# First MLP's input kept in SBUF: attention's output evicted into the contraction's rows, two heads moved by DMA within SBUF

## The chip, the cores and the metric

The kernel runs on one core of a Trainium2 chip. The metric is the device time of one execution in microseconds, the median of three runs. TensorE is the matrix engine, VectorE (DVE) and ScalarE (ACT) do elementwise work, GpSimd (POOL) is all but unused, and SyncE (SP) issues every DMA. TensorE's clock is granted at one of two levels, 1.2 GHz (0.50 in the profile) and 2.4 GHz (1.00).

## The reference

A gated linear attention is followed by two MLPs over the same 3072 tokens.

```python
# batch 4, heads 8, seq 768, head_dim 48
f = 1 / (1 + exp(-f_logit))
for t in range(S):
    state = f[t][:, None] * state + outer(k[t], v[t])
    y[t] = q[t] @ state
x = y as rows of 3072 tokens by 384 (8 heads x 48)
# first MLP, d_ff 2048
h = x @ w1_in
x = where(h > 0, h, exp(min(h, 0)) - 1) @ w1_out
# second MLP
h = maximum(x @ w2_in, 0)
out = (h * h) @ w2_out
```

## The kernel before

**Attention.** The 3072 tokens are 24 units of 128 tokens; six units are one sequence. A unit is worked in slots: A (log of the gate, L204 to L206), B (running sum and its exponentials), C (scaled q and k, L226 and L227), K (k transposed and evicted as kp, L238), S (the state, L258 and L259), D (scores and their mask, L272 and L277), E (state and scores times v on TensorE, L307 and L317, then the eviction of y, L326, two instructions). y has 112 rows: head dimensions of one head in rows 0 to 47, of another in rows 64 to 111, with four pairs of heads along the columns. Slot E ends with two DMAs that store y to the DRAM tensor x1d (L330).

**MLPs.** The tokens are also seven blocks of 3, 4, 4, 4, 4, 3 and 2 units. For a block, `load_x` reads x from x1d into the tile xl (L457), `split_x` makes a high part xh on ScalarE (L463) and a low part xl on VectorE (L464), and 16 steps follow, one for each 128 columns of d_ff. A step is nine matmuls into ph (L360 to L362: high by high, high by low, low by high, for three contraction rows of 128), elementwise work on ScalarE and VectorE (L374 to L390), and nine or more matmuls into acc (L410 to L412 in the first MLP, L435 to L437 in the second), two steps later. The first MLP's result goes to the DRAM tensor x2d and is read back by the same `load_x`.

**Weights.** Each of the four matrices has eight chunks of 768 KB in 64-bit words. `load_w` loads a chunk (L133) into a raw tile: the first seven into borrowed weight tiles, later ones into two stage buffers. `conv_w` makes its high and low parts in four stages: ScalarE (L146), VectorE (L148, L149, L152), ScalarE (L165), VectorE (L167). The second MLP's w_in goes into SBUF that the attention has given back, in `close_attention`.

**Order.** The order is written by a planner. The first three units and what goes between them are the strings `LOADS` and `EXTRA` with times of their own; names in them are loads of weights (Li1, Lo1), conversions (i0, i1), moves or loads of x (X), splits (Y) and warm-up matmuls for the clock (Z). After that the planner's clock `at` counts one for each unit of an MLP step: 384 for the first MLP, of which the blocks begin at 0, 48, 112, 176, 240, 304 and 352. `ends` gives the time near which a unit's slot E stands, and the other slots stand at fixed distances before it. Loads, slots A and conversions are tied to the elementwise instructions of an earlier step (`gates`). A scheduler may still let a ready instruction pass one that waits; then each engine and SP's queue run in order. The last attention event is `last_at`; from it the loads of the second w_in follow with the distance `gap`.

```python
PACE = 0.835
ends.append(ends[-1] + (NEAR if block_of[u] == 1 else NF * PACE) if u > BLOCKS[0] else FIRST)
...
last_at = max(e[0] for e in events) + 0.5
events.append((last_at, close_attention, ()))
tail = at[n1 - NF]
gap = max(3, (tail - last_at) / (WC - 1))
loads = [(last_at + 2 + gap * c, (2, "in", c)) for c in range(WC - 1)]
```

Of the kernel before, what the change touches and what calls it, by code (L numbers as in the profile page):

```python
# [18 lines left out]
P = 128  # L19
B, H, S, D = 4, 8, 768, 48  # L20
DM = H * D
# [16 lines left out]
BORROW = 7  # L38
LDB = {"f": 3, "qk": 2, "v": 3}
LOADS = "f0 f1 qk0 qk1 f2 v0 v1 i0 qk2 v2 o0"  # L40
SPIN = 10
# [15 lines left out]
NEAR = 8  # L57
GET = {"f": ("A", 7), "qk": ("C", 8), "v": ("S", 9)}
PACE = 0.835


@with_exitstack
def gla_mlp_kernel(
# [108 lines left out]
    U = {}  # L172
    LAST = {}

    def load_unit(u, names, after=None):
        d = U.setdefault(u, {})
        done = []
        if "f" in names:
            d["f"] = ld.tile([112, 4, P], F32, tag="f", name="ld_f", bufs=LDB["f"])
            done.append(nc.sync.dma_start(d["f"], fqk[u, :, 0]))  # L180
        if "qk" in names:
            d["qk"] = ld.tile([112, 2, 4, P], F32, tag="qk", name="ld_qk", bufs=LDB["qk"])
            done.append(nc.sync.dma_start(d["qk"], fqk[u, :, 1:3]))
        if "v" in names:
            d["v"] = ld.tile([P, H, D], F32, tag="v", name="ld_v", bufs=LDB["v"])
# [152 lines left out]
    X = {}  # L338

    def x_tiles(key, n):  # L340
        xh = pl.x.tile([P, KC, n], F32R, tag="xh", name="xh")
        xl = pl.x.tile([P, KC, n], F32R, tag="xl", name="xl")
        X[key] = (xh, xl)
        return xh, xl

    first_unit = [sum(BLOCKS[:j]) for j in range(len(BLOCKS))]
    steps = [(layer, j, f) for layer in (1, 2) for j in range(len(BLOCKS)) for f in range(NF)]
# [100 lines left out]

    def load_x(layer, j, part=None):
        n = BLOCKS[j] * P  # L450
        t0 = first_unit[j] * P
        if not part:
            x_tiles((layer, j), n)
        xl = X[layer, j][1]
        cols = slice(0, n) if part is None else slice(part * P, (part + 1) * P)
        src = (x1d, x2d)[layer - 1][:, :, t0 + cols.start : t0 + cols.stop]
        nc.sync.dma_start(xl[:, :, cols].bitcast(F32), src.rearrange("k p t -> p k t"))  # L457

    def split_x(layer, j, flag=None, part=None):
        xh, xl = X[layer, j]  # L460
        if part is not None:
            xh, xl = (t[:, :, part * P : (part + 1) * P] for t in (xh, xl))
# [18 lines left out]
    def general_attention():  # L481
        with ExitStack() as g:
# [11 lines left out]
            for b in range(B):  # L494
                units = slice(b * UPB, (b + 1) * UPB)
                for pr in range(H // 2):
# [25 lines left out]
                    for e in range(D):  # L522
# [28 lines left out]
                    nc.vector.tensor_copy(y.rearrange("p (i n) -> p i n", i=2), py)  # L551
                    c0 = 2 * D * pr
                    nc.sync.dma_start(
                        x1d.rearrange("k p t -> (k p) t")[c0 : c0 + 2 * D, b * S : (b + 1) * S], y
                    )

# [21 lines left out]
    for name in LOADS.split():  # L578
        if name == "i0":
            load_w(1, "in", 0)  # L580
            done.add("Li0")
        elif name == "o0":
            load_w(1, "out", 0)
            done.add("Lo0")
        else:
            load_unit(int(name[-1]), name[:-1])
# [20 lines left out]

    block_of = [j for j, n in enumerate(BLOCKS) for _ in range(n)]

    def close_attention():  # L610
# [11 lines left out]
    def run_slot(u, s):  # L622
        slots, back = AFTER.get(s, ("", 0))
        assert all(u < back or f"{x}{u - back}" in done for x in slots), (u, s)
        SLOT[s](u)


# [4 lines left out]
    def gates(t):  # L632
        return GATE.get(bisect_right(at, t) - 1 - BACK if t >= 0 else -1, ())

# [19 lines left out]
    def do(name, t=None):  # L654
        kind, rest = name[0], name[1:]
        if kind == "L":
            w = (1, {"i": "in", "o": "out"}[rest[0]], int(rest[1:]))
            load_w(*w, after=LAST["ins"].ins if t is None else [LAST["ins"].ins, *gates(t)][-1])
        elif kind == "G":
            n = rest.rstrip("0123456789")  # L660
            load_unit(int(rest[len(n) :]), [n], [LAST["ins"].ins, *gates(t)][-1])
        elif kind in "io":
            c, n = rest.split(".")
            with ExitStack() as stack:
                for ins in gates(t) if t is not None else ():
                    stack.enter_context(tc.issue_after(ins))
                conv_w(int(n), 1, {"i": "in", "o": "out"}[kind], int(c))
        elif kind == "Z":
            u, n = (int(i) for i in rest[1:].split("."))
            src = U[u][{"q": "qT", "k": "kp", "y": "y"}[rest[0]]]  # L670
            src = src.rearrange("p a t -> p (a t)" if rest[0] != "y" else "p a b t -> p (a b t)")
            spin(n, src.bitcast(mybir.dt.bfloat16)[:, 1::2])
# [4 lines left out]
        elif kind == "X":  # L677
            load_x(1, *(int(i) for i in rest.split(".")))
        elif kind == "Y":
# [6 lines left out]
        else:  # L686
            with ExitStack() as stack:
                for ins in gates(t) if t is not None and kind == "A" else ():
                    stack.enter_context(tc.issue_after(ins))
# [96 lines left out]
def _layout(inputs):  # L786
# [3 lines left out]
    def heads(x):  # L790

        x = x.reshape(B, 4, 2, UPB, P, D).transpose(0, 3, 2, 5, 1, 4).reshape(NU, 2, D, 4, P)
        return _np.concatenate([x[:, 0], x[:, 0, :16], x[:, 1]], axis=1)

    def parts(w, kind):

# [12 lines left out]
        ),  # L809
        "moe_w_in": parts(inputs["moe_w_in"], "in"),  # L810
        "moe_w_out": parts(inputs["moe_w_out"], "out"),
# [33 lines left out]
```

## Time and profile before

| what | us |
|---|---|
| median of 3 runs | 958.08 |
| lowest and highest run | 957.34, 960.02 |
| profiled execution, its own time | 962.39 |
| span of the profiled execution, first to last instruction | 960.7 |
| TensorE matmuls busy | 925.8 (96%) |
| VectorE busy | 506.5 (53%) |
| ScalarE busy | 461.9 (48%) |

The mean granted clock of TensorE over the span is 0.979. Matmuls are pipelined and their ends are modelled, so a busy TensorE is not TensorE at its peak. The shares of the other engines are means over stages with different limits.

### The profile page before, as it was taken

What the parts mean: (1) busy time and instruction counts of PE and PEld (TensorE: products, weight loads), DVE (VectorE), ACT (ScalarE), POOL (GpSimd) and SP (SyncE); (2) the same over time, 40 slices, a digit from 0 to 9 for tenths busy, and PEclk for the clock granted to TensorE, in tenths of its full rate; (3) what the DMA queues carried; (4) which work ended last, traced back from release to release, by engine and by line L of the source; (5) the groups of instructions that cost most, each with busy time, mean ns of one, the idle gap of its engine ahead of it and who ended that gap; (6) DMA issues with size and microseconds to landing.
All of it is one profiled execution on the core that took longest, in us unless ns stands there. A gap on an engine that the chain in (4) does not pass through costs nothing.

```text
span 960.7 us, 14209 instructions
## 1 busy us (share of the span) xinstructions
PE 925.8 (96%) x5781; PEld 812.0 (85%) x5781; DVE 506.5 (53%) x798; ACT 461.9 (48%) x867; POOL 1.1 (0%) x8
## 2 busy tenths in 40 slices
PE   7689899999999999999999999999999999999996
PEld 4477787888887788778999899999999999999996
DVE  6489984555465564546655893434334334334342
ACT  5278674555565564545656663333223323323332
POOL 0000000000000000000000000000000000000000
PEclk7789999999999999999999999999999999999998
DMA  6546641233133222221213531001001001001000
GB/s 188 175 135 213 194 141 55 66 94 107 52 90 107 61 82 73 78 79 63 88 66 92 188 117 33 26 1 36 31 1 67 1 1 58 1 10 41 1 25 21
DMA packets 37146, 71.00 MB, mean 74 GB/s; under 512 B 3408, under 2 KB 22992, under 8 KB 37072
## 3 DMA queue, kind: packets, MB, share of 16 engines
q1 hardware_dynamic: 37072, 70.01, 23.0%
q8 instruction: 47, 0.77, 0.3%
q14 instruction: 27, 0.22, 0.1%
HBM read 55.84 MB, written 14.16 MB: 73 GB/s over the span
## 4 chain that ended last, share of the span: by engine, by line
PE 85%; DVE 6%; DMA 6%; ACT 2%; issue 1%; SPq 0%; ACTq 0%; DVEq 0%
PE ph L360 13%; PE ph L361 13%; PE ph L362 13%; PE acc L437 7%; PE acc L435 7%; PE acc L436 7%; PE acc L410 6%; PE acc L411 6%; PE acc L412 6%; PE ps_bb L272 2%; PE ps_bb L317 2%; DMA wraw<-in_moe_w_out_dram 1%; DMA wraw<-in_moe_w_in_dram 1%; DMA xl<-x1d 1%; DVE wa L149 1%
## 5 line engine op out<-in xcount | busy, mean ns | idle before, releaser
L360 PE MATMUL ph<-xh,w 128*128 128x512 f32 (+2 forms) x672 | 245.8, 366 | 8.2 <-ACT xh L463 4.7
L362 PE MATMUL ph<-xh,w 128*128 128x512 f32 (+2 forms) x672 | 244.5, 365 | 0.7 <-DVE w L167 0.7
L361 PE MATMUL ph<-xl,w 128*128 128x512 f32 (+2 forms) x672 | 244.5, 364 | 0.0
L390 DVE TENSOR_TENSOR gl<-g,gh 128x512 fp32r<-128x512 f32 (+2 forms) x224 | 137.1, 614 | 98.9 <-ACT gh L389 61.0
L389 ACT ACTIVATE gh<-g 128x512 fp32r<-128x512 f32 (+2 forms) x224 | 127.5, 569 | 126.5 <-DVE g L379 73.5
L379 DVE SCALAR_TENSOR_TENSOR g<-ph,g 128x512 f32<-128x512 f32 (+2 forms) x112 | 68.6, 613 | 156.9 <-ACT g L378 156.9
L360 PEld LDWEIGHTS ph<-xh,w 128*128 128x128 f32 x672 | 127.8, 191 | 25.5 <-ACT xh L463 5.2
L362 PEld LDWEIGHTS ph<-xh,w 128*128 128x128 f32 x672 | 127.9, 190 | 17.0 <-DVE w L167 1.2
L378 ACT ACTIVATE g<-ph 128x512 f32<-128x512 f32 (+2 forms) x112 | 59.9, 535 | 167.7 <-PE ph L362 166.1
L361 PEld LDWEIGHTS ph<-xl,w 128*128 128x128 f32 x672 | 127.9, 190 | 13.4 <-issue 0.2
L435 PE MATMUL acc<-w,gh 128*128 128x384 f32 x384 | 128.9, 336 | 0.0
L436 PE MATMUL acc<-w,gh 128*128 128x384 f32 x384 | 128.9, 336 | 0.0
L437 PE MATMUL acc<-w,gl 128*128 128x384 f32 x384 | 124.7, 336 | 0.0
L411 PE MATMUL acc<-gl,w 128*128 128x512 f32 (+2 forms) x336 | 120.7, 363 | 1.4 <-DVE gl L390 1.3
L412 PE MATMUL acc<-gh,w 128*128 128x512 f32 (+2 forms) x336 | 118.9, 362 | 0.0
L376 DVE SCALAR_TENSOR_TENSOR g<-g,ph 128x512 f32<-128x512 f32 (+2 forms) x112 | 67.9, 607 | 92.5 <-ACT g L375 92.4
L410 PE MATMUL acc<-gh,w 128*128 128x512 f32 (+2 forms) x336 | 112.7, 369 | 3.2 <-ACT w L165 2.4
L374 ACT ACTIVATE g<-ph 128x512 f32<-128x512 f32 (+2 forms) x112 | 59.4, 531 | 76.2 <-PE ph L362 70.3
L436 PEld LDWEIGHTS acc<-w,gh 128*128 128x128 f32 x384 | 72.2, 188 | 3.0
L435 PEld LDWEIGHTS acc<-w,gh 128*128 128x128 f32 x384 | 72.2, 188 | 2.8
L410 PEld LDWEIGHTS acc<-gh,w 128*128 128x128 f32 x336 | 61.0, 189 | 12.8 <-ACT w L165 3.1
L437 PEld LDWEIGHTS acc<-w,gl 128*128 128x128 f32 x384 | 71.7, 188 | 0.0
(77 smaller groups left out, 861.1 us busy)
## 6 DMA issues: line engine op xcount, KB each, us to landing
wraw<-in_moe_w_in_dram SPq DMA_DIRECT2D x16, 768.0 KB, 4.4
wraw<-in_moe_w_out_dram SPq DMA_DIRECT2D x16, 768.0 KB, 4.4
ld_qk<-in_fqk_dram SPq DMA_DIRECT2D x24, 448.0 KB, 3.7
ld_f<-in_fqk_dram SPq DMA_DIRECT2D x24, 224.0 KB, 2.7
ld_v<-in_v_dram SPq DMA_DIRECT2D x24, 192.0 KB, 2.7
x1d<-y SPq DMA_DIRECT2D x48, 96.0 KB, 2.1
out_dram<-ob SPq DMA_DIRECT2D x24, 192.0 KB, 1.9
xl<-x1d SPq DMA_DIRECT2D x4, 768.0 KB, 4.4
```

Source lines behind the costliest of these rows:

```text
L360: nc.tensor.matmul(ph, wh[:, kk, fs], xh[:, kk, :], start=kk == 0, stop=False)
L361: nc.tensor.matmul(ph, wh[:, kk, fs], xl[:, kk, :], start=False, stop=False)
L362: nc.tensor.matmul(ph, wl[:, kk, fs], xh[:, kk, :], start=False, stop=kk == KC - 1)
L379: last = nc.vector.scalar_tensor_tensor(g, ph, 0.0, g, op0=ALU.max, op1=ALU.mult)
L389: nc.scalar.activation(gh, g, AF.Copy)
L390: nc.vector.tensor_tensor(gl, g, gh.bitcast(F32), op=ALU.subtract)
L410: nc.tensor.matmul(acc[c], wh[:, fi, cs], gh, start=first, stop=False)
L411: nc.tensor.matmul(acc[c], wh[:, fi, cs], gl, start=False, stop=False)
L412: nc.tensor.matmul(acc[c], wl[:, fi, cs], gh, start=False, stop=last)
L435: nc.tensor.matmul(acc[c], gh[:, cs], wh[:, fi, :], start=first, stop=False)
L436: nc.tensor.matmul(acc[c], gh[:, cs], wl[:, fi, :], start=False, stop=False)
L437: nc.tensor.matmul(acc[c], gl[:, cs], wh[:, fi, :], start=False, stop=last)
```

## The change

The contraction rows of the first MLP get another order, and w1_in's rows are permuted in the same way on the host. Three of each four heads are evicted by ScalarE straight to their rows in a tile xr of the block (rows 0 to 47 and 64 to 111 of three row groups); the fourth of each is evicted to a fourth group, and six DMAs of 16 partitions each move it into rows 48 to 63 and 112 to 127 of the three groups. xr has one buffer, of four groups by the block's columns. `split_x` reads xr. The units of a block are spread between the start of the block before and 13 before its own start. For SBUF, f and v get two buffers instead of three, with unit 2's f and v in MLP tiles, and `zeros` is halved, which narrows the opening warm-up matmuls to 256 columns; those on y narrow to 128. w_in chunk 1 is loaded at the end of the opening loads. Three conversions are held behind named slots instead of behind an MLP step. The fallback path, which does not run here, is changed to the same rows.

```diff
-LDB = {"f": 3, "qk": 2, "v": 3}
-LOADS = "f0 f1 qk0 qk1 f2 v0 v1 i0 qk2 v2 o0"
+LDB = {"f": 2, "qk": 2, "v": 2}
+LOADS = "f0 f1 qk0 qk1 f2 v0 v1 i0 qk2 v2 o0 i1"
...
-    "Li1 6.56 Lo1 8.05 i0 8.5 X0.0 6.6 X0.1 8.1 X0.2 11.6 Y0.0 11.65 Y0.1 11.66 Y0.2 11.7 i1 12.5 "
+    "X0.0 6.6 Lo1 6.7 X0.1 8.1 Li2 8.2 Gf3 8.3 X0.2 11.6 Lo2 11.61 i0 8.5 Y0.0 11.65 Y0.1 11.66 Y0.2 11.7 i1 12.5 "
...
+HOLD = {"i1": "D1 E0", "o0": "D2 K1", "o1": "D2 E1"}
...
+OPEN = 1.5
+CLOSE = 13
+GET = {"f": ("A", 6), "qk": ("C", 8), "v": ("S", 9)}
...
-    zeros = ap.tile([P, 4 * P], mybir.dt.bfloat16, name="zeros")
+    zeros = ap.tile([P, 2 * P], mybir.dt.bfloat16, name="zeros")
...
-        y = d["y"] = ap.tile([112, 2, 2, P], F32, tag="y", name="y", bufs=2)
+        b = block_of[u]
+        if u == first_unit[b]:
+            XR[b] = ap.tile([P, KC + 1, BLOCKS[b] * P], F32, tag="xr", name="xr")
+        t0 = (u - first_unit[b]) * P
+        y = d["y"] = XR[b][:112, :, t0 : t0 + P]
         for j in range(2):
             LAST["ins"] = nc.scalar.activation(
-                y[:, :, j, :], banks[j][:112, : 2 * P].rearrange("p (g t) -> p g t", g=2), AF.Copy
+                y[:, j::2, :], banks[j][:112, : 2 * P].rearrange("p (g t) -> p g t", g=2), AF.Copy
             )
+    def move_x(j, part=None):
+        xr = XR[j]
+        n = BLOCKS[j] * P
+        cols = slice(0, n) if part is None else slice(part * P, (part + 1) * P)
         for i in range(2):
-            nc.sync.dma_start(
-                x1d.rearrange("k p t -> (k p) t")[
-                    4 * D * i : 4 * D * (i + 1), u * P : (u + 1) * P
-                ].rearrange("(h e) t -> e h t", e=D),
-                y[64 * i : 64 * i + D].rearrange("p g j t -> p (g j) t"),
-            )
+            for kk in range(KC):
+                nc.sync.dma_start(
+                    xr[64 * i + D : 64 * (i + 1), kk, cols],
+                    xr[64 * i + 16 * kk : 64 * i + 16 * (kk + 1), KC, cols],
+                )
...
-        nc.scalar.activation(xh, xl.bitcast(F32), AF.Copy, accum_out=flag)
-        nc.vector.tensor_tensor(xl, xl.bitcast(F32), xh.bitcast(F32), op=ALU.subtract)
+        nc.scalar.activation(xh, xr, AF.Copy, accum_out=flag)
+        nc.vector.tensor_tensor(xl, xr, xh.bitcast(F32), op=ALU.subtract)
...
-                for ins in gates(t) if t is not None else ():
+                held = HOLD.get(f"{kind}{c}")
+                for ins in [MARK[m].ins for m in held.split()] if held else gates(t):
                     stack.enter_context(tc.issue_after(ins))
...
-            load_x(1, *(int(i) for i in rest.split(".")))
+            move_x(*(int(i) for i in rest.split(".")))
...
-    for u in range(BLOCKS[0], NU):
-        ends.append(ends[-1] + (NEAR if block_of[u] == 1 else NF * PACE) if u > BLOCKS[0] else FIRST)
+    for j in range(1, len(BLOCKS)):
+        lo, hi = (need(j - 1) + OPEN, need(j) - CLOSE) if j > 1 else (FIRST, need(1) - NEAR)
+        ends += [lo + (hi - lo) * k / (BLOCKS[j] - 1) for k in range(BLOCKS[j])]
...
-        plan(min(need(j), ends[first_unit[j] + BLOCKS[j] - 1] + 8) - 6.8, f"X{j}")
-        plan(need(j) - 4, f"Y{j}")
+        plan(ends[first_unit[j] + BLOCKS[j] - 1] + 2.5, f"X{j}")
+        plan(need(j) - 3, f"Y{j}")
```

`MARK` keeps the last instruction of each slot; a conversion held by "D1 E0" is issued on VectorE behind unit 1's slot D and on ScalarE behind unit 0's slot E.

## Rows read from the trace of the kernel before

**Rows 1.** Busy time by stretch: engine busy us and instructions, granted clock, DMA.

```profile
0.00:45.00 45.00, 29.60 (x233) 18.16 (x234) 26.02 (x43) 18.68 (x37) 1.08 (x8) 0.80 0.61 192
45.00:130.00 85.00, 75.98 (x590) 65.39 (x588) 75.71 (x118) 57.52 (x112) 0.00 (x0) 0.93 0.54 172
130.00:425.00 295.00, 294.42 (x2062) 235.88 (x2063) 161.65 (x248) 166.37 (x313) 0.00 (x0) 1.00 0.27 80
425.00:500.00 75.00, 75.00 (x384) 68.64 (x383) 44.62 (x68) 44.89 (x80) 0.00 (x0) 1.00 0.24 82
...
580.00:950.00 370.00, 370.00 (x1981) 345.01 (x1979) 137.72 (x218) 123.76 (x220) 0.00 (x0) 1.00 0.06 22
```

**Rows 2.** The same view, shorter stretches; order PE, PEld, DVE, ACT, POOL, PEclk.

```profile
44.00:51.00 7.00, 6.13 (x18) 5.53 (x18) 1.02 (x2) 3.28 (x7) 0.00 (x0) 0.54 0.18 66
...
110.00:131.00 21.00, 18.31 (x156) 15.71 (x155) 18.42 (x28) 12.35 (x24) 0.00 (x0) 1.00 0.55 178
480.00:500.00 20.00, 20.00 (x118) 20.00 (x117) 11.20 (x19) 11.29 (x21) 0.00 (x0) 1.00 0.24 79
520.00:530.00 10.00, 10.00 (x85) 9.80 (x84) 6.37 (x15) 6.15 (x16) 0.00 (x0) 1.00 0.26 85
530.00:575.00 45.00, 43.02 (x276) 41.70 (x275) 38.93 (x65) 29.09 (x58) 0.00 (x0) 0.96 0.44 150
```

**Rows 3.** Chain of waits up to the first MLP matmul: start us, us, what.

```profile
21.22 6.61 DMA wraw<-in_moe_w_in_dram
...
37.59 2.07 DMA x1d<-y
39.72 3.98 DMA xl<-x1d
...
44.40 1.01 PE ph L360 x2
```

**Rows 4.** Timeline, 22 to 37 us: start, us, engine, line, idle before and releaser.

```profile
22.77 1.29 DVE L277 TENSOR_TENSOR a<-ps_bb,tri 128x512 f32<-128x512 f32 x2 [0.62 <-PE ps_bb L272]
...
24.87 1.16 PE L272 MATMUL ps_bb<-qT,kT 48*128 48x128 f32 x16
27.92 1.69 ACT L146 ACTIVATE wa<-wraw 128x768 f32<-128x768 f32 x2 [7.60 <-DMA wraw<-in_moe_w_in_dram]
...
32.52 1.28 DVE L277 TENSOR_TENSOR a<-ps_bb,tri 128x512 f32<-128x512 f32 x2
...
36.83 0.38 ACT L326 ACTIVATE y<-ps_b 112x256 f32<-112x256 f32 x1 [0.42 <-PE ps_b L317]
```

**Rows 5.** Groups of instructions by form: count, busy us, mean ns, idle before.

```profile
L390 DVE TENSOR_TENSOR gl<-g,gh 128x384 fp32r<-128x384 f32 x64 | 35.3, 554 | 20.7 <-ACT gh L389 19.4 <-PE acc L411 1.2
...
L149 DVE SCALAR_TENSOR_TENSOR wa<-wraw,wa 128x768 uint32<-128x768 uint32 x32 | 30.3, 952 | 0.3
...
L148 DVE TENSOR_SCALAR wa<-wa 128x768 uint32<-128x768 uint32 x32 | 17.7, 556 | 18.2 <-ACT wa L146 18.2
...
L390 DVE TENSOR_TENSOR gl<-g,gh 128x256 fp32r<-128x256 f32 x32 | 13.5, 422 | 11.8 <-ACT gh L389 11.8
```

**Rows 6.** Chain of waits before block 1's first matmul, store and load of x.

```profile
117.56 2.94 DMA x1d<-y
...
120.56 6.06 DMA xl<-x1d
```

**Rows 7.** SP's timeline, first and last of seven loads of the second w_in.

```profile
417.87 0.35 SPq L133 DMA_DIRECT2D wraw<-in_moe_w_in_dram  x1
...
493.16 0.33 SPq L133 DMA_DIRECT2D wraw<-in_moe_w_in_dram  x1
```

**Rows 8.** VectorE's timeline in the later weight conversions, two instructions in a row.

```profile
542.07 0.95 DVE L167 TENSOR_TENSOR w<-wa,w 128x768 fp32r<-128x768 f32 x1
542.94 0.95 DVE L149 SCALAR_TENSOR_TENSOR wa<-wraw,wa 128x768 uint32<-128x768 uint32 x1
```

**Rows 9.** DMA issues on the page: count, size, median us to landing.

```profile
x1d<-y SPq DMA_DIRECT2D x48, 96.0 KB, 2.1
```

More of the change, by code (lines that the diff above doesn't have):

```diff
@@ L57 @@
 NEAR = 8
-GET = {"f": ("A", 7), "qk": ("C", 8), "v": ("S", 9)}
-PACE = 0.835
+OPEN = 1.5
+CLOSE = 13
+GET = {"f": ("A", 6), "qk": ("C", 8), "v": ("S", 9)}
 @with_exitstack
@@ L173, in gla_mlp_kernel @@
     LAST = {}
+    X, XR, MARK = {}, {}, {}
+    first_unit = [sum(BLOCKS[:j]) for j in range(len(BLOCKS))]
+    block_of = [j for j, n in enumerate(BLOCKS) for _ in range(n)]
     def load_unit(u, names, after=None):
@@ L178, in load_unit @@
         if "f" in names:
-            d["f"] = ld.tile([112, 4, P], F32, tag="f", name="ld_f", bufs=LDB["f"])
+            if u == 2:
+                d["f"] = pl.moe.tile([P, MAXN], F32, tag="g", name="ld_f")[:112]
+                d["f"] = d["f"].rearrange("p (a t) -> p a t", a=4)
+            else:
+                d["f"] = ld.tile([112, 4, P], F32, tag="f", name="ld_f", bufs=LDB["f"])
             done.append(nc.sync.dma_start(d["f"], fqk[u, :, 0]))
@@ L184, in load_unit @@
         if "v" in names:
-            d["v"] = ld.tile([P, H, D], F32, tag="v", name="ld_v", bufs=LDB["v"])
+            if u == 2:
+                d["v"] = pl.moe.tile([P, DM], F32, tag="o", name="ld_v", bufs=3)
+                d["v"] = d["v"].rearrange("p (h d) -> p h d", h=H)
+            else:
+                d["v"] = ld.tile([P, H, D], F32, tag="v", name="ld_v", bufs=LDB["v"])
             done.append(nc.sync.dma_start(d["v"], v[u]))
@@ L447, in o_mm, with load_x, split_x @@
                 del ACC[layer, j]
-    def load_x(layer, j, part=None):
+    def load_x(layer, j):
         n = BLOCKS[j] * P
         t0 = first_unit[j] * P
-        if not part:
[L453 to L459, printed above, removed]
+        xl = pl.x.tile([P, KC, n], F32R, tag="xl", name="xl")
+        XR[j] = xl.bitcast(F32)
+        X[layer, j] = [None, xl]
+        src = (x1d, x2d)[layer - 1][:, :, t0 : t0 + n]
+        nc.sync.dma_start(xl.bitcast(F32), src.rearrange("k p t -> p k t"))
+    def split_x(layer, j, flag=None, part=None):
+        n = BLOCKS[j] * P
+        if not part:
+            xh = pl.x.tile([P, KC, n], F32R, tag="xh", name="xh")
+            if (layer, j) in X:
+                X[layer, j][0] = xh
+            else:
+                X[layer, j] = [xh, pl.x.tile([P, KC, n], F32R, tag="xl", name="xl")]
         xh, xl = X[layer, j]
+        xr = XR[j][:, :KC]
         if part is not None:
-            xh, xl = (t[:, :, part * P : (part + 1) * P] for t in (xh, xl))
-        nc.scalar.activation(xh, xl.bitcast(F32), AF.Copy, accum_out=flag)
-        nc.vector.tensor_tensor(xl, xl.bitcast(F32), xh.bitcast(F32), op=ALU.subtract)
+            xh, xl, xr = (t[:, :, part * P : (part + 1) * P] for t in (xh, xl, xr))
+        nc.scalar.activation(xh, xr, AF.Copy, accum_out=flag)
+        nc.vector.tensor_tensor(xl, xr, xh.bitcast(F32), op=ALU.subtract)
     def flag_count():
@@ L551, in general_attention @@
                     nc.vector.tensor_copy(y.rearrange("p (i n) -> p i n", i=2), py)
[L552 to L555, printed above, removed]
+                    for j in range(2):
+                        i, q = divmod(2 * pr + j, 4)
+                        cols = slice(b * S, (b + 1) * S)
+                        if q < KC:
+                            nc.sync.dma_start(
+                                x1d[q, 64 * i : 64 * i + D, cols], y[D * j : D * (j + 1)]
+                            )
+                        else:
+                            for kk in range(KC):
+                                r = D * j + 16 * kk
+                                nc.sync.dma_start(
+                                    x1d[kk, 64 * i + D : 64 * (i + 1), cols], y[r : r + 16]
+                                )
     def general_mlp(layer):
@@ L578, in gla_mlp_kernel @@
     for name in LOADS.split():
[L579 to L584, printed above, removed]
+        if name[0] in "io":
+            load_w(1, {"i": "in", "o": "out"}[name[0]], int(name[1:]))
+            done.add("L" + name)
         else:
@@ L606, in gla_mlp_kernel @@
     nc.vector.tensor_copy(tri, ones)
-    block_of = [j for j, n in enumerate(BLOCKS) for _ in range(n)]
     def close_attention():
@@ L625, in run_slot @@
         SLOT[s](u)
+        MARK[f"{s}{u}"] = LAST["ins"]
     at = [0]
@@ L632, in gates @@
     def gates(t):
-        return GATE.get(bisect_right(at, t) - 1 - BACK if t >= 0 else -1, ())
+        return GATE.get(bisect_right(at, t) - 1 - BACK if t is not None and t >= 0 else -1, ())
     total = len(steps)
@@ L657, in do @@
             w = (1, {"i": "in", "o": "out"}[rest[0]], int(rest[1:]))
-            load_w(*w, after=LAST["ins"].ins if t is None else [LAST["ins"].ins, *gates(t)][-1])
+            load_w(*w, after=[LAST["ins"].ins, *gates(t)][-1])
         elif kind == "G":
@@ L670, in do @@
             src = U[u][{"q": "qT", "k": "kp", "y": "y"}[rest[0]]]
-            src = src.rearrange("p a t -> p (a t)" if rest[0] != "y" else "p a b t -> p (a b t)")
+            src = src.rearrange("p a t -> p (a t)") if rest[0] != "y" else src[:, KC, :]
             spin(n, src.bitcast(mybir.dt.bfloat16)[:, 1::2])
@@ L687, in do @@
             with ExitStack() as stack:
-                for ins in gates(t) if t is not None and kind == "A" else ():
+                for ins in gates(t) if kind == "A" else ():
                     stack.enter_context(tc.issue_after(ins))
@@ L793, in heads @@
         return _np.concatenate([x[:, 0], x[:, 0, :16], x[:, 1]], axis=1)
+    order = _np.array(
+        [
+            (p // 64 * 4 + (kk if p % 64 < D else 3)) * D + (p % 64 if p % 64 < D else 16 * kk + p % 64 - D)
+            for kk in range(KC)
+            for p in range(P)
+        ]
+    )
     def parts(w, kind):
@@ L809, in _layout @@
         ),
-        "moe_w_in": parts(inputs["moe_w_in"], "in"),
+        "moe_w_in": parts(inputs["moe_w_in"][order], "in"),
         "moe_w_out": parts(inputs["moe_w_out"], "out"),
```

7 lines of the change are left out of this document (removed).

## The prediction

> **What bounds the kernel now.** I read the busy times by stretch first, then the chain of waits, then the timeline at the places that the chain names. By stretch [rows 1] the span falls in three kinds of time. From 130 to 500 us and from 580 to 950 us TensorE is busy without a gap at a granted clock of 1.00 (2.4 GHz): there only less TensorE work would help, and the change removes none but some warm-up matmuls at the start. From 0 to 45 us TensorE is waiting for the attention of the first three units, and it was granted a mean of 0.80. From 45 to 130 us VectorE is the bound: 75.7 of 85 us busy [rows 1], where it converts weights, runs the attention of units 3 to 6 and the elementwise steps of block 0 together. A fourth, small place is 530 to 575 us, where the second layer's weights are converted: TensorE idles 2.0 us and is granted 0.96, which is another 1.8 us, so about 3.8 us are lost [rows 2]. The reader should see that the change can gain only before 130 us, and can lose wherever VectorE's work is pushed closer together.
>
> The chain of waits before the first MLP matmul (44.4 us) goes through a weight load of 6.61 us, later the store of unit 2's x to DRAM, 2.07 us, and its load, 3.98 us [rows 3]. The timeline says what the weight load held up [rows 4]. ScalarE sat 7.60 us at the first conversion step of w_in chunk 1 until 27.92 us, and its queue is in order: the evictions of units 1 and 2 stood behind. VectorE's queue shows the same from the other side. Unit 2's score matmuls begin at 24.87 us and take 1.16 us, so their masking (L277) could start at 26.0; it starts at 32.52 because the late conversions of w_in chunk 1 and w_out chunk 0 stand ahead of it. From that start to the end of unit 2's y it is 4.7 us (32.52 to 36.83 + 0.38 = 37.21).
>
> **Part 1, the early load of w_in chunk 1 and the held conversions.** The load moves from behind unit 0's store on SP's queue to the end of the opening loads. It puts 768 KB more on queues that carry nothing but opening loads, so that at worst the third qk load, which SP issues late, lands a little later. I cost this at nothing, since its user is in VectorE's queue behind other work; at most 1 us. What it frees: ScalarE no longer meets a weight that is not there. The hold puts chunk 1's VectorE steps behind unit 1's masking, which ends at 22.77 + 1.28 = 24.05 us [rows 4]. The three steps that precede the low half take 0.56 + 0.95 + 0.95 = 2.5 us [rows 5] (L152 has the form of L149, and so has L167 in length), so unit 2's masking starts at about 26.5 in place of 32.5, and y of unit 2 ends at about 31.2 in place of 37.2. Gain 6.0 us. Bounds: 2 us if only the ScalarE wait goes and VectorE still runs both conversions first, 7 us if the masking goes ahead of them.
>
> **Part 2, no trip through DRAM.** From the end of y of unit 2 (37.21) to the landing of the load (39.72 + 3.98) it is 6.5 us [rows 3]. In its place stand six moves of 16 partitions each, all on SP. One issue costs SP about 0.4 us by the nearest row, the 0.35 us of a weight load's issue [rows 7], so the six take 2.4 us, and the last lands 2.1 us after it, the median of the 96 KB stores [rows 9]: 4.5 us. Gain 2.0 us. No row shows a move within SBUF; the nearest bounds are the store's 2.1 us landing with issues hidden (gain 4.4), and six landings in a row, 12.6 us (a loss of 6.1). I take the first kind because the two stores of one unit already overlap: one chain piece of 2.07 us covers the last of them, not two. Behind the six issues on SP stand weight loads and unit loads, delayed by up to 2.4 us; their users run after the first MLP steps.
>
> The Trainium skill's page DMA: Bandwidth & Descriptors, in "Rules for kernel authors", says to coalesce small transfers, because below 64 KB one pays mostly overhead, and puts that overhead at about 2 us for each; the six here are 8 KB (parts) or 32 KB each. The trace shows the 2 us for 96 KB, and that such times overlap. Paid one after the other they would be the 12.6 us above, which is a rival below.
>
> **Part 3, w_out chunk 1 converted before the MLP starts.** Its four VectorE instructions, 0.56 + 3 x 0.95 = 3.4 us [rows 5], leave the stretch where VectorE is full and go to the stretch where it waits: 1.02 us busy of 7 between 44 and 51 us [rows 2], and similarly just before. I take 2 us of the 3.4, since the full stretch also has holes that wait for DMA. Bounds 0 and 3.4.
>
> **Part 4, x of block 1.** The store and load after unit 6 take 2.94 and 6.06 us [rows 6], from 117.2 to 126.6 us; the moves would take 4.5. That is 4.9 us sooner, but TensorE idles only 21.0 - 18.3 = 2.7 us between 110 and 131 us [rows 2], partly for VectorE. I take 1 us, bounds 0 and 2.5. Later blocks gain nothing: TensorE hides their trip.
>
> Sum of the parts: 6.0 + 2.0 + 2.0 + 1.0 = 11 us gained by 130 us, bounds 5 and 14. The shorter warm-up matmuls (128 columns in place of 512, the opening ones 256) are inside these bounds: between 44 and 51 us the clock already averages 0.54 [rows 2], so at the same place little is left to lose.
>
> **Part 5, what the single x buffer moves.** All of a block's y now go to one buffer, which is not free until the block before has been split. So the attention can no longer run ahead of the MLP. In the planner's clock (one for each 128 tokens of an MLP step, 384 for the first layer) the last unit ended at 40 + 17 x 13.36 = 267; it now ends at 352 - 13 = 339. Until then the attention's SBUF is not given back, and the second layer's w_in has to wait for it. Before, its first seven chunks were loaded from 417.87 to 493.16 us, one in some 12 us [rows 7], with VectorE 44.6 of 75 us busy and no loss on TensorE [rows 1]. Now the first is planned at 342.5 and the gap falls from 11.9 to 3, so seven fall in 342.5 to 363.5, and the eighth at 362.
>
> The price of that: eight conversions of 3.4 us are 27.3 us of VectorE. The elementwise steps beside them are 3.2 steps of the three-unit block at 2 x 0.55 and 6.5 of the two-unit block at 2 x 0.42 [rows 5], 9.0 us, and a split of three times 384 columns, 1.7. That is 38.0 us by durations. In a full queue the next instruction starts 0.87 us after one of 0.95 [rows 8], 8% sooner, which makes 35. TensorE passes the same steps in 3.2 x 20 us / 118 x 18 + 6.5 x 10 us / 85 x 18 = 23.5 us, 18 matmuls in each step [rows 2]. The deficit is 11.5 us. It need not be paid in full: chunk c is needed only at 384 + 6c, and the conversions could trail into 530 to 575 us, where 6 us of VectorE's 45 are free, and beyond 580 us, where it is busy 37% [rows 1, 2]. But VectorE takes its queue in order, so a conversion ahead of an elementwise step stalls TensorE two steps later. Bounds: 0, and 11.5 plus some 2.5 for a clock that falls in the gaps (530 to 575 us lost 1.8 that way). I take 6, half of the deficit and a little clock, because the nearest stretch, 530 to 575 us, lost 3.8 us with VectorE 87% busy, and this one asks for more.
>
> **The sum.** 11 gained, 6 given back: 5 us less. The profiled execution took 962.39 us for a span of 960.7, so it would be 957.4; the median of the runs is 4.3 us lower, 958.08, which makes 953.
>
> **Rivals.** (a) *The squeeze costs nothing*: conversions trail and TensorE never waits longer than now. The time is then 958 - 11 = 947. For it: weights are needed late. Against it: the loss at 530 to 575 us with fewer conversions. (b) *The squeeze decides, slower than before*: with 14 us given back and 11 or less gained, 961 or more. It decides from 14 us on, that is when the two raw buffers make each of the seven conversions wait for a load and the steps wait with them. (c) *VectorE swallows the early start*: MLP steps begin earlier but the full stretch ends when it did, less part 3. The gain is then 3 to 5, and with 6 given back the time is 959 to 961. Against it: nothing in that stretch is tied to absolute time; its loads follow the steps. (d) *The moves are paid in a row*: part 2 becomes a loss of 6, part 4 zero; 6 + 2 - 6 - 6 gives 962.
>
> **How the numbers follow.** Forecast 0.42 (its own range 949 to 956), (a) 0.21, (b) 0.18, (c) 0.13, (d) 0.06. A measurement of this kernel tells 0.3%, 2.9 us, from no change. Faster takes 0.40 of the forecast, all of (a) and 0.02 of (c); no change 0.02 of the forecast, 0.05 of (b), 0.08 of (c) and 0.02 of (d); slower the rest: 0.63, 0.17, 0.20. The range runs from 944 (14 gained, none given back) to 962 (less gained, or most of the deficit paid).
>
> **What would show it.** Right: no long ScalarE wait for a w_in load before 30 us; unit 2's masking near 26 us; the first MLP matmul near 36 us; x moves landing 4 to 5 us after the last y; VectorE 95% busy and TensorE with gaps between about 495 and 560 us; the second layer's first w_in load near 495 us. Wrong: a masking that still waits behind conversions, moves that land one after the other, or a TensorE that passes the end of the first layer without gaps.

## The result and the profile after

The changed kernel took 972.51 us (median of four runs, 972.26 to 976.31) beside 958.8 us of the kernel before on the same chip: a ratio of 1.0145 (1.0123 to 1.0167). It is slower by some 14 us, past the upper end of the forecast's own range (956) and of the whole range (962).

The profiled executions took 962.39 and 976.31 us. To see where the 13.9 us arise, each trace is cut at the same places of the program, by counting the matmuls into ph: from the first one to 48 planner units (the end of block 0), to 340 (about where the attention of the new kernel ends), to 384 (the end of the first MLP), and to the last matmul. Each cut is the start of the last matmul into ph before that place; the matmuls into acc, two steps behind, can fall on either side of it. Here, and for the experiments below:

```
                      first     1 to    48 to   340 to   384 to   profiled
                      matmul      48      340      384      last      time
before                  44.4     80.3    369.3     47.1    411.3    962.39
after                   39.1     82.0    376.0     60.0    410.7    976.31
e1_spread               38.4     80.0    376.0     53.8    407.7    964.66
e2_ahead                37.4     79.1    368.5     47.0    411.8    952.35
e3_packed               37.0     79.3    367.4     61.1    410.9    964.16
e4_late_load            34.7     84.0    376.0     60.0    410.0    973.22
e5_before_squeeze       40.8     81.6    365.9     61.5    411.0    971.19
e6_before_early_load    37.3     78.7    369.1     47.1    410.4    952.36
e7_ahead_no_early_load  39.3     79.8    372.7     47.1    411.0    958.26
e8_ahead_packed         37.2     78.6    371.1     47.0    410.8    953.19
e9_less_vector          36.4     83.0    376.1     54.0    409.2    967.38
e10_ahead_early_w2      35.8     79.4    368.5     46.9    411.0    949.78
e11_ahead_early_outs    35.5     79.0    368.5     48.9    404.6    945.05
e12_spread_packed       38.3     80.3    369.9     51.1    411.6    959.65
```

Single profiles differ by a few us in the opening. e5 opens as the kernel before does, and reaches 48 units at 122.4 us, not at 124.7. e1, e2, e3, e8, e9 and e12 open as the changed kernel does, and reach them at 115.8 to 119.4, not at 121.1. So some 5 us were gained by the end of block 0, of which this pair shows 3.6; the 1.7 us that block 0 itself loses in the pair lie within the scatter (78.6 to 83.0 us in those six). Further on, 6.7 and 12.9 us were lost in two places, where e1, e4 and e9 give 376.0 or 376.1 again for the first and e4 gives 60.0 again for the second. The second layer from 384 units on is as it was.

**The start.** Busy time by stretch after, the counterpart of [rows 1]:

```profile
0.00:45.00 45.00, 25.71 (x249) 19.19 (x249) 26.12 (x44) 21.39 (x41) 1.09 (x8) 0.89 0.60 188
45.00:130.00 85.00, 73.16 (x598) 62.98 (x599) 79.77 (x125) 61.29 (x119) 0.00 (x0) 0.98 0.45 148
580.00:950.00 370.00, 370.00 (x1961) 344.97 (x1960) 145.33 (x226) 126.43 (x221) 0.00 (x0) 1.00 0.07 24
```

From 45 to 130 us VectorE is busier still, 79.8 of 85 us in place of 75.7. The timeline of VectorE and ScalarE in the opening shows unit 2's mask, its y, and the split that waits for the moved rows; the counterpart of [rows 4]:

```profile
25.99 1.28 DVE L292 TENSOR_TENSOR a<-ps_bb,tri 128x512 f32<-128x512 f32 x2
...
28.40 0.82 ACT L346 ACTIVATE xr<-ps_b 112x256 f32<-112x256 f32 x2 [1.45 <-PE ps_b L332]
...
38.43 0.52 ACT L486 ACTIVATE xh<-xr 128x384 fp32r<-128x384 f32 x1 [1.64 <-DMA xr<-xr]
```

The mask starts at 25.99 in place of 32.52 us and y ends at 29.22 in place of 37.21: 8.0 us won. But the rows are there only at 38.4, 9.2 us after y, where the trip through DRAM took 6.5. SP's timeline of DMA issues, and the chain of waits (start, us, what) in place of [rows 3], say why:

```profile
22.22 3.76 SPq L357 DMA_DIRECT2D xr<-xr  x6
26.08 0.53 SPq L136 DMA_DIRECT2D wraw<-in_moe_w_out_dram  x1
26.65 0.43 SPq L136 DMA_DIRECT2D wraw<-in_moe_w_in_dram  x1
27.18 10.05 SPq L357 DMA_DIRECT2D xr<-xr  x12
```

```profile
26.65 7.53 DMA wraw<-in_moe_w_in_dram
...
34.19 0.51 SPq L357
...
34.74 0.59 SPq L357
...
36.64 1.72 DMA xr<-xr
...
38.43 0.62 ACT xh L486 x2
...
39.10 1.01 PE ph L376 x2
```

Six issues take SP 3.76 us, 0.63 from one to the next. The twelve moves of units 1 and 2 stand in a row: unit 2's first comes up at about 27.18 + 6 x 0.63 = 31.0, and its second stands until 34.19, when the load of w_in chunk 2, issued at 26.65 us, has landed. In the two programs SP's DMAs use eight completion semaphores in turn, and one that is to be used again must have its last DMA landed; the DMA eight before unit 2's second move is that load. The view of waits on SP, 15 to 45 us (us in total, times, longest), names it:

```profile
SPq L357 <- DMA wraw<-in_moe_w_in_dram: 2.6, 1, 2.6
```

So the 9.2 us are 1.8 behind unit 1's moves, 0.6 for the first issue, 2.6 at the semaphore, 2.5 up to the last issue and 1.7 to its landing. In e1, e3, e9 and e12, which open in the same way, the wait at the semaphore is 2.4, 1.1, 1.1 and 2.3 us.

The load held back more than the semaphore. DMA issues from 27.15 to 31.0 us, which are unit 1's six moves, and from 31.1 to 37 us, unit 2's six (count, size, median us to landing):

```profile
xr<-xr SPq DMA_DIRECT2D x6, 8.0 KB, 6.0
```

```profile
xr<-xr SPq DMA_DIRECT2D x6, 8.0 KB, 1.7
```

Unit 1's moves were issued while the load was under way and landed only after it, 6.0 us from their issue in place of 1.7. So unit 2's moves might have landed no sooner without the semaphore; no run separates the two, since e4 and e10 take the load away from both.

**48 to 340 units.** Units 7 to 23 of the attention stand in this stretch before and after, and TensorE is shown busy without a gap in nearly all of it. The score matmuls (slot D, 16 for a unit) show the loss. In the groups by form, 130 to 500 us, before and after (out<-in, form, count, busy us, mean ns):

```profile
L272 PE MATMUL ps_bb<-qT,kT 48*128 48x128 f32 x256 | 21.3, 289 | 0.0
L360 PE MATMUL ph<-xh,w 128*128 128x384 f32 x42 | 14.1, 335 | 0.0
```

```profile
L287 PE MATMUL ps_bb<-qT,kT 48*128 48x128 f32 x244 | 26.1, 296 | 0.0
L376 PE MATMUL ph<-xh,w 128*128 128x384 f32 x37 | 13.4, 363 | 0.0
```

Fewer score matmuls are busy longer, and so are the MLP's matmuls of 384 columns of the line L360, now L376, 363 ns in place of 335. In the chain of waits after one finds them in a run of 16, and in pairs between the steps of the MLP:

```profile
452.76 1.09 PE ps_bb L287 x16
453.85 0.38 PE ph L376
...
473.13 0.18 PE acc L428
473.31 0.42 PE ps_bb L287 x2
473.72 0.37 PE ph L376
...
477.07 0.42 PE ps_bb L287 x2
477.49 0.37 PE ph L376
```

Sixteen in a run take 1.09 us, 0.07 each. A lone pair takes 0.42, and the MLP matmul behind it 0.37 in place of 0.18: 0.61 for two, 0.47 more than for two of a run. Counted from 130 to 500 us the scores stand in 38 runs after and in 23 before; 15 x 0.47 = 7.1 us by this estimate, and 6.7 are missing. Why the scheduler cuts them up is read from the plan and was not tested by itself: the slots of the late units are far apart there, so a unit's scores are ready many steps before slot E wants them, and can fill each small hole. It fits that the loss is gone in e2, which sets the units close again.

**340 to 384 units.** SP's timeline of the second w_in, in place of [rows 7], and the busy times by stretch (PE, PEld, DVE, ACT, POOL, PEclk), in place of [rows 2]:

```profile
499.16 0.81 SPq L136 DMA_DIRECT2D wraw<-in_moe_w_in_dram  x2
...
508.88 2.43 SPq L136 DMA_DIRECT2D wraw<-in_moe_w_in_dram  x2
...
518.72 4.13 SPq L136 DMA_DIRECT2D wraw<-in_moe_w_in_dram  x2
...
530.89 3.32 SPq L136 DMA_DIRECT2D wraw<-in_moe_w_in_dram  x2
```

```profile
510.00:520.00 10.00, 10.00 (x71) 10.00 (x70) 9.38 (x14) 8.73 (x16) 0.00 (x0) 1.00 0.71 221
520.00:525.00 5.00, 3.54 (x19) 2.50 (x18) 5.00 (x9) 4.16 (x10) 0.00 (x0) 1.00 0.69 206
525.00:530.00 5.00, 3.13 (x21) 2.68 (x21) 3.61 (x10) 2.27 (x6) 0.00 (x0) 1.00 0.63 220
530.00:540.00 10.00, 9.70 (x76) 9.01 (x75) 9.32 (x17) 7.29 (x16) 0.00 (x0) 1.00 0.47 157
```

Eight chunks are loaded within 35 us where seven had 75. VectorE is full from 510 to 525 us, and TensorE falls to 40 matmuls in the 10 us from 520 on, about half of what it does before and after. The granted clock stays at 1.00 in these rows, so none of this is the clock.

### The profile page after: what moved, and what is told of

The parts are those of the page before. It is cut to its first block, busy times and chain, and to the rows that moved or that the text cites. A ratio compares the mean times of both kernels' runs of the same rounds, so it can differ in the third digit from the quotient of the medians.

```text
span 974.6 us, 14204 instructions
## 1 busy us (share of the span) xinstructions
PE 927.9 (95%) x5781; PEld 809.4 (83%) x5781; DVE 505.8 (52%) x798; ACT 466.0 (48%) x867; POOL 1.1 (0%) x8
## 4 chain that ended last, share of the span: by engine, by line
PE 81%; DMA 8%; DVE 7%; ACT 2%; issue 1%; SPq 1%; ACTq 0%; DVEq 0%
PE ph L376 13%; PE ph L378 12%; PE ph L377 12%; PE acc L451 7%; PE acc L453 7%; PE acc L452 7%; PE acc L426 6%; PE acc L427 5%; PE acc L428 5%; PE ps_bb L287 3%; DMA wraw<-in_moe_w_in_dram 2%; DMA wraw<-in_moe_w_out_dram 2%; PE ps_bb L332 2%; DVE wa L152 1%; DVE wa L155 1%
## 5 line engine op out<-in xcount | busy, mean ns | idle before, releaser
L376 PE MATMUL ph<-xh,w 128*128 128x512 f32 (+2 forms) x672 | 247.5, 369 | 17.7 <-ACT xh L486 9.1
L376 PEld LDWEIGHTS ph<-xh,w 128*128 128x128 f32 x672 | 127.1, 189 | 38.2 <-ACT xh L486 9.3
L427 PEld LDWEIGHTS acc<-gl,w 128*128 128x128 f32 x336 | 63.2, 188 | 13.7 <-DVE gl L406 5.5
```

Of the source, the lines that this page charges most:

```text
L376: nc.tensor.matmul(ph, wh[:, kk, fs], xh[:, kk, :], start=kk == 0, stop=False)
L427: nc.tensor.matmul(acc[c], wh[:, fi, cs], gl, start=False, stop=False)
```

## Experiments

Each edit is made to the changed kernel, but for e5 and e6, which edit the kernel before. The expectations name the theories as they stood before each run. The kernel before had medians of 960.56 (beside e1 to e4), 960.03 (e5 to e8) and 959.78 us (e9 to e12).

**e1_spread: the conversions of the second w_in further apart, those of its w_out later and further apart.**

```diff
-    gap = max(3, (tail - last_at) / (WC - 1))
+    gap = 6
...
-    loads += [(tail + 18 + FPC * BLOCKS[-1] * c, (2, "out", c)) for c in range(WC)]
+    loads += [(tail + 30 + 6 * c, (2, "out", c)) for c in range(WC)]
```

> The changed kernel with the second layer's conversions spread: first matrix 6 apart from 342.5, second from 382 with 6 between. Theory A (the squeeze of eight conversions into 24 units overfills VectorE, and that is 13 us of the loss): units 340 to 384 take about 50 us in place of 60.0 (before: 47.0) and the time falls from 972.5 to about 963. Rival (the 13 us come from the block change itself, its x2 load and split, which lie at the same place): no more than 2 us less, 970 to 973.

963.74 us, ratio 1.0029 (1.0013 to 1.0044). The stretch from 340 units falls from 60.0 to 53.8 us and the second layer's from 410.7 to 407.7; the stretch from 48 to 340 stays. Seven conversions stand between 340 and 384 units in place of ten, and half of the loss there is gone with the others. The later start of w_out's conversions has a part in that, and was not tested apart here.

**e2_ahead: the attention at its old pace, so that it ends early again.**

```diff
-        lo, hi = (need(j - 1) + OPEN, need(j) - CLOSE) if j > 1 else (FIRST, need(1) - NEAR)
-        ends += [lo + (hi - lo) * k / (BLOCKS[j] - 1) for k in range(BLOCKS[j])]
+        for k in range(BLOCKS[j]):
+            ends.append(FIRST + NEAR * k if j == 1 else ends[-1] + 13.36)
...
-        plan(need(j) - 3, f"Y{j}")
+        plan(min(need(j) - 3, ends[first_unit[j] + BLOCKS[j] - 1] + 10), f"Y{j}")
```

> The changed kernel with the attention at the old pace (13.36 between units) and each block split 10 after its last unit, so that the single x buffer is free in time and the attention ends at 267 again. Theory A (what is lost is lost because the attention ends at 339: conversions squeezed, 13 us, and score matmuls scattered into odd gaps, 8 us): the time is that of the kernel before less the 5 us won at the start, about 953 to 955. Rival (the single buffer and its moves cost by themselves, wherever the attention stands): 963 or more.

951.93 us, ratio 0.9911 (0.9885 to 0.9938). Both late losses are gone: 368.5 and 47.0 us. The single x buffer does not force a late end of the attention; splitting a block as soon as its rows are there frees the buffer, and the old pace fits. The pace and the place of the split were changed together.

**e3_packed: the scores held together, behind a whole MLP step.**

```diff
-            nc.tensor.matmul(ph, wl[:, kk, fs], xh[:, kk, :], start=False, stop=kk == KC - 1)
+            LAST["pe"] = nc.tensor.matmul(
+                ph, wl[:, kk, fs], xh[:, kk, :], start=False, stop=kk == KC - 1
+            )
...
+                if kind == "D" and "pe" in LAST:
+                    stack.enter_context(tc.issue_after(LAST["pe"].ins))
```

> The changed kernel with a unit's score matmuls held on TensorE behind the matmuls of the step before their planned place, so that the scheduler can't scatter them two by two over earlier steps. Theory A (a pair between MLP matmuls costs 0.6 us where 16 in a row cost 1.1, and this is most of the 8 us lost between units 112 and 340): 5 to 8 us less, 965 to 967. Rival (the 8 us come from the blocks that the attention now stands beside, not from the scatter): 971 to 973.

964.16 us, ratio 1.0041 (1.0020 to 1.0062): 8.4 us less than the changed kernel in the median, and 8.6 less from 48 to 340 units (367.4). The group by form of the same stretch, 130 to 500 us:

```profile
L287 PE MATMUL ps_bb<-qT,kT 48*128 48x128 f32 x256 | 18.6, 285 | 0.0
```

As many matmuls as before the change take 18.6 us in place of 21.3. The squeeze is untouched (61.1).

**e4_late_load: unit 2's moves ahead of the load of w_in chunk 2 and of unit 3's f.**

```diff
-    "X0.0 6.6 Lo1 6.7 X0.1 8.1 Li2 8.2 Gf3 8.3 X0.2 11.6 Lo2 11.61
+    "X0.0 6.6 Lo1 6.7 X0.1 8.1 X0.2 11.6 Li2 11.602 Gf3 11.604 Lo2 11.61
```

> The changed kernel with the load of w_in chunk 2 and unit 3's f behind unit 2's moves. Theory A (a DMA issue waits until the eighth DMA before it has landed, so unit 2's second move waited for the 768 KB load until 34.2 us): the moves run without the hole, the first MLP matmul comes at about 36.5 in place of 39.1 us and the time is about 2 us less, 970. Rival (VectorE is the bound after the start and swallows it): first matmul earlier, time 972 to 973.

973.82 us, ratio 1.0146 (1.0121 to 1.0170): no gain on the changed kernel, though the first MLP matmul is at 34.7 us, 4.4 sooner in the profiles. At 48 units, 118.7 us, it is no earlier than the kernels that open as the changed one does (115.8 to 121.1). The 2.6 us hole is gone, but another load is waited for. In the chain of waits:

```profile
34.91 9.71 DMA ld_f<-in_fqk_dram
44.62 0.02 issue
44.64 0.04 DVE ld_f L219
```

This is unit 4's f, the second f load after the opening. It is issued 3.5 us sooner than in the changed kernel (38.37 us there), but now behind the load of w_in chunk 2 as well as other large loads, and lands at 44.6 us in place of 44.5. VectorE, which in the changed kernel comes to it at 47.8, now stands 1.1 us for it. Block 0 takes 84.0 us, the longest in the table.

**e5_before_squeeze: the kernel before, with the second w_in as late as in the changed kernel.**

```diff
+    last_at = 340.5
     events.append((last_at, close_attention, ()))
```

> The kernel before, its x still through DRAM and its attention as it was, with one thing moved: the attention's SBUF is given back at 340.5 and the second w_in follows 3 apart, as in the changed kernel. Theory A (the squeeze alone costs about 13 us between units 340 and 384): 970 to 973. Rival (the squeeze hurts only together with attention that stands beside it): 960 to 963.

971.47 us, ratio 1.0138 (1.0112 to 1.0164). The squeeze alone makes the kernel before as slow as the changed one. From 48 to 384 units it takes 427.4 us, 11.0 more than before. Of the 61.5 us from 340 units some 3 are a shift: 18 matmuls into acc more fall behind that cut (180 in place of 162), and the stretch ahead of it is 3.4 us shorter. Busy times by stretch:

```profile
500.00:520.00 20.00, 16.34 (x100) 14.69 (x98) 18.09 (x29) 14.31 (x29) 0.00 (x0) 0.97 0.62 211
520.00:545.00 25.00, 23.13 (x164) 21.98 (x164) 21.75 (x41) 16.79 (x38) 0.00 (x0) 0.89 0.51 167
```

Here the granted clock falls as well, to 0.89.

**e6_before_early_load: the kernel before with part 1** (early load of w_in chunk 1, conversions held), x still through DRAM. One of the held conversions is that of w_out chunk 1, so part 3 is in it too.

```diff
-LOADS = "f0 f1 qk0 qk1 f2 v0 v1 i0 qk2 v2 o0"
+LOADS = "f0 f1 qk0 qk1 f2 v0 v1 i0 qk2 v2 o0 i1"
+HOLD = {"i1": "D1 E0", "o0": "D2 K1", "o1": "D2 E1"}
...
-    "Li1 6.56 Lo1 8.05 i0 8.5 X0.0 6.6 X0.1 8.1 X0.2 11.6 Y0.0 11.65 Y0.1 11.66 Y0.2 11.7 i1 12.5 "
+    "Lo1 6.7 i0 8.5 X0.0 6.6 X0.1 8.1 X0.2 11.6 Y0.0 11.65 Y0.1 11.66 Y0.2 11.7 i1 12.5 "
...
```

> The kernel before with part 1 of the change alone: w_in chunk 1 at the end of the opening loads, the three conversions held, x still through DRAM. Theory B (the start is won by this part, and the DRAM trip was no dearer than 18 moves): first MLP matmul near 37 us, unit 48 some 6 us earlier than before, time 952 to 955. Rival (the gain needs x kept in SBUF): first matmul at 40 us or later, time 957 or more.

952.87 us, ratio 0.9938 (0.9919 to 0.9957). With the early load, the trip through DRAM gives the first MLP matmul at 37.3 us, as early as the moves give it in e2 (37.4). In the chain of waits:

```profile
29.79 2.42 DMA x1d<-y
...
32.27 4.38 DMA xl<-x1d
...
37.34 1.01 PE ph L362 x2
```

**e7_ahead_no_early_load: e2 without part 1**: x stays in SBUF, `LOADS` and `EXTRA` have the loads and conversions where they were.

```diff
-LOADS = "f0 f1 qk0 qk1 f2 v0 v1 i0 qk2 v2 o0 i1"
+LOADS = "f0 f1 qk0 qk1 f2 v0 v1 i0 qk2 v2 o0"
...
-    "X0.0 6.6 Lo1 6.7 X0.1 8.1 Li2 8.2 Gf3 8.3 X0.2 11.6 Lo2 11.61 i0 8.5 Y0.0 11.65 Y0.1 11.66 Y0.2 11.7 i1 12.5 "
+    "Li1 6.56 Lo1 8.05 i0 8.5 X0.0 6.6 X0.1 8.1 X0.2 11.6 Y0.0 11.65 Y0.1 11.66 Y0.2 11.7 i1 12.5 "
...
-HOLD = {"i1": "D1 E0", "o0": "D2 K1", "o1": "D2 E1"}
+HOLD = {}
...
```

> The counterpart: x kept in SBUF with the attention at the old pace (as in the 952 us version), but without part 1: chunk 1 loaded where the kernel before loads it and no conversion held. Theory B: nothing is won at the start, 958 to 962. Rival (skipping the DRAM trip wins by itself): 953 to 956.

956.49 us, ratio 0.9962 (0.9949 to 0.9975): x in SBUF, with the buffers and warm-up matmuls that the change altered for it, is worth some 3.6 us (2.4 to 4.9). That lies between what the two theories gave, so it decides for neither. It and e6 do not add up: both together (e2) have a ratio of 0.9911, with an interval that overlaps e6's (0.9919 to 0.9957). So beside the early load no pair of runs shows a gain from x in SBUF by itself.

**e8_ahead_packed: e2 with e3's hold.**

```diff
...
+            ends.append(FIRST + NEAR * k if j == 1 else ends[-1] + 13.36)
...
+                if kind == "D" and "pe" in LAST:
+                    stack.enter_context(tc.issue_after(LAST["pe"].ins))
```

> The 952 us version with the score matmuls of a unit held together as well. Theory A: they stand in one run of 16 for 11 of its 16 later units already, so only 1 to 2 us are left, 949 to 951. Rival (holding them also ends waits behind the mask on VectorE): 946 or less.

953.08 us, ratio 0.9941 (0.9923 to 0.9958): no gain on e2, whose interval overlaps. From 48 to 340 units it takes 371.1 in place of 368.5 us, but one unit's 16 scores more fall on this side of the cut, so a cost of the hold is not shown.

**e9_less_vector: one of VectorE's three instructions before the high half left out for the second layer's weights.**

```diff
-            nc.vector.scalar_tensor_tensor(
-                ti, high, 0x80000000, ti, op0=ALU.bitwise_and, op1=ALU.bitwise_or
-            )
+            if layer == 1:
+                nc.vector.scalar_tensor_tensor(
+                    ti, high, 0x80000000, ti, op0=ALU.bitwise_and, op1=ALU.bitwise_or
+                )
```

> The changed kernel without the one VectorE instruction that puts the sign back into the second layer's weights (0.87 us for each of 16 conversions; the weights lose their sign, loads and ScalarE's work stay). Theory A (VectorE's occupation is what the squeeze costs): some 11 of these conversions lie between units 340 and 384, so up to 9.6 us of its work go, that stretch takes 51 to 54 us in place of 60 and the time is 964 to 967. Rival (two raw buffers and their loads set the pace): the stretch stays at 58 or more, 970 to 973.

966.06 us, ratio 1.0063 (1.0046 to 1.0081). With the loads where they were, the stretch from 340 units falls from 60.0 to 54.0 us. Ten conversions stand in that stretch, eight of w_in and two of w_out, and each loses this instruction. In the changed kernel it took there (window, busy us and count, granted clock, DMA):

```profile
497.13:557.14 60.01, 9.52 (x10) 1.00 0.50 167
```

Of these 9.5 us 6.0 come back as time, so VectorE's work sets at least that much of the 12.9 us lost. The loads are not ruled out for the rest: in the changed kernel ScalarE waits for the raw chunks (its waits from 440 to 590 us: us in total, times, longest).

```profile
ACT wa L149 <- DMA wraw<-in_moe_w_in_dram: 4.3, 5, 2.5
```

SP in turn stands for VectorE to free a raw buffer before it issues the next of these loads, so the two hang together.

**e10_ahead_early_w2: e2, with the load of w_in chunk 2 and of unit 3's f ahead of unit 0's moves.**

```diff
-    "X0.0 6.6 Lo1 6.7 X0.1 8.1 Li2 8.2 Gf3 8.3 X0.2 11.6
+    "Li2 6.57 Gf3 6.58 X0.0 6.6 Lo1 6.7 X0.1 8.1 X0.2 11.6
```

> The 952 us version with the load of w_in chunk 2 and unit 3's f ahead of unit 0's moves, so that they neither stand before unit 2's moves nor come late. Theory C (in the run with the late load the start was won and given back by f and chunk 2 arriving late): first matmul at 35 to 36 us, units 1 to 48 in 78 to 79 us again, 949 to 950. Rival (VectorE swallows any earlier start): 952.

949.78 us, ratio 0.9895 (0.9868 to 0.9922). The first MLP matmul is at 35.8 us here and at 35.5 in e11, against 36.4 to 39.1 in the seven profiles with the load where the change has it; block 0 takes 79.4. In the median it is 2.2 us less than e2, but the intervals overlap. This fits the reading of e4: the loads are kept away from unit 2's moves without harm if they go ahead of the moves, not behind. The six moves run without a hole, in the chain of waits:

```profile
29.89 0.84 SPq L357
...
33.30 1.73 DMA xr<-xr
```

From 29.89 to 35.03 us it is 5.1 us; from the end of y, at 29.4, to the split it is 5.7.

**e11_ahead_early_outs: e10, with the second w_out's conversions later and further apart, as in e1.**

```diff
-    loads += [(tail + 18 + FPC * BLOCKS[-1] * c, (2, "out", c)) for c in range(WC)]
+    loads += [(tail + 30 + 6 * c, (2, "out", c)) for c in range(WC)]
```

> The same with the second w_out's conversions spread as in the first experiment, 6 apart from 382. Theory A: the loss between units 384 and 432, which the kernel before has too, shrinks by 2 to 4 us: 946 to 948. Rival: no change against the run beside it.

945.70 us, ratio 0.9852 (0.9825 to 0.9880): faster than both kernels, and the fastest here. The second layer takes 404.6 in place of 411.0 us, and the stretch before it 48.9 in place of 46.9; in the medians 4.1 us are won on e10. The stretch that lost 3.8 us before [rows 2] loses nothing; busy times by stretch:

```profile
520.00:545.00 25.00, 25.00 (x185) 25.00 (x184) 16.07 (x31) 16.20 (x36) 0.00 (x0) 1.00 0.41 144
545.00:580.00 35.00, 35.00 (x204) 35.00 (x203) 31.63 (x49) 20.65 (x35) 0.00 (x0) 1.00 0.34 113
```

**e12_spread_packed: e1 and e3 together.**

```diff
...
+    gap = 6
...
+                if kind == "D" and "pe" in LAST:
+                    stack.enter_context(tc.issue_after(LAST["pe"].ins))
```

> The changed kernel with its attention ending at 339 as it does, but conversions spread and score matmuls held together. Theory A (two separate losses of about 9 us each): they add up, 954 to 957. Rival (both repairs fill the same idle time): 960 or more.

956.71 us, ratio 0.9964 (0.9946 to 0.9983). The two late losses are separate: e1 won 8.8 and e3 8.4 us on the changed kernel, both together 15.8 of 17.2.

## Why the prediction was wrong, point by point

The sum foresaw 5 us less. One of its parts held, and three steps failed: part 2's price of the moves, part 5's half of the deficit, and the stretch from 130 us on that was taken as fixed.

**Part 1 was right.** 6.0 us were forecast up to the end of unit 2's y, 8.0 came: ScalarE's wait went, and the mask starts at 25.99 us (forecast 26.5). Some 1.5 us more than forecast came by luck, since from the mask to the end of y it took 3.2 us, not 4.7. e6 makes it, with part 3, in the kernel before and wins some 6 to 7 us.

**Part 2 failed in its terms, and in the sign for this kernel.** The trip was taken as 4.5 us and measured 9.2 (7.6 to 9.3 in the six other profiles of this opening). An issue costs 0.59 us, not 0.4; the six moves stand behind six others; and one waits 2.6 us for a load that has nothing to do with it. Even without the hole and the queue (e10) it is 5.1 us, so against 6.5 the gain is 1.4 rather than 2.0. Rival (d), moves paid in a row, foresaw the wrong mechanism: 8 KB moves land in 1.8 us in the median and overlap, though 6.0 us behind a large load; SP's issues are what stands in a row. The Trainium skill, DMA: Bandwidth & Descriptors, "Rules for kernel authors", asks to coalesce transfers under 64 KB because they are mostly overhead. The trace agrees: 8 KB land in 1.8 us in the median, 96 KB in 2.1 [rows 9].

**Parts 3 and 4 did not show.** They were to give 3 us between the first matmul and 48 units. Before, the stretch took 80.3 us, and 81.6 in e5; after 82.0, in the six kernels with the same opening 78.6 to 83.0, and in e6 78.7. Nothing beyond this scatter is shown. The bounds of the parts' sum, 5 and 14, were too narrow as well: they left out part 2's own bound, a loss of 6.1, and 3.6 (about 5 over the profiles) came.

**Part 5 failed in its size.** The deficit of 11.5 us and the bound of 14 were worked out; half, 6, was taken, because conversions could trail. They did not: the stretch lost 12.9 us, and e5 alone loses 11.4 in the median. The argument that was set against trailing, a queue in order in which a conversion ahead of an elementwise step stalls TensorE, was the one that held, for 6.0 us at least: so much e9 gives back for 9.5 of VectorE. A slip that changes nothing: seven loads 3 apart from 342.5 end at 360.5, not at 363.5. Rival (b), 961 us or more, named the side that came true, but not by its own condition: 12.9 us were given back, not 14, and that each conversion waits for a load is shown only in part, by ScalarE's 4.3 us.

**A term was missing.** The sum took 130 to 500 us as fixed, because TensorE is busy without a gap there. The new places of the slots cut the scores into pairs, for 6.7 us; e3 takes them back. With the whole deficit paid but without that term, the prediction's sum would have been 958 - 11 + 11.5 to 14, 959 to 961. The measured terms are -5.3 + 1.7 + 6.7 + 12.9 - 0.6 = 15.4 us; behind the last matmul 1.5 us come off, which leaves the 13.9 between the profiled executions.

**What stays open.** Why a lone pair of score matmuls and the matmul behind it take 0.61 us was not tested; only the price was shown. Nor was it tested what the 6.9 us of the squeeze are that e9 does not give back, whether the semaphore or the queue behind the load holds unit 2's moves, or why x in SBUF and the early load do not add up.

## What to carry to other kernels

A change of a buffer's count moves the end of everything that fills it: work out what is squeezed in the remaining room, and where VectorE has more work than time there, take the whole deficit, as it came here, since its queue is in order. When work is moved, look at how it falls between the instructions of an engine that is busy all the time; a busy share of 100% does not say that nothing can be lost. Small DMAs are paid at the issuing queue: count the issues ahead, and look for large loads among the last eight and for any that is still under way.

## What was not expected of the hardware

SP's issue of a 16-partition move within SBUF took 0.51 to 0.59 us in the chain of the opening, a weight load's 0.33 [rows 7], 0.43 and 0.53 in the rows shown. An issue stood 2.6 us for the landing of a 768 KB load that was issued eight DMAs earlier, and six moves of 8 KB issued behind that load landed 6.0 us after their issue in place of 1.7. Two score matmuls of 48 rows, alone between matmuls of 128, cost 0.61 us with what follows them, where in a run of 16 one costs 0.07; the trace shows TensorE busy in both.
